# A gated recurrence and a multiplicative FFN on one core: the bf16 cast moves from VectorE to GpSimd, and the second half of the output copy from VectorE to ScalarE

## The chip, the core and the metric

The kernel runs on one core of a Trainium2 chip. The core has five engines that each work through a list of instructions in order and meet only at semaphores: TensorE (matmuls; PE in the profile, and PEld for its weight loads), VectorE (DVE), ScalarE (ACT), GpSimd (POOL) and SyncE (SP, which here only issues transfers). Sixteen DMA engines move data between the device memory (DRAM) and the on-chip SBUF. TensorE writes its results into a second on-chip memory, PSUM, from which VectorE or ScalarE have to copy them out. The metric is the time of one execution on the device in microseconds (us), lower being better.

## What is computed

A recurrence over the sequence, with learned gates, and then a feed-forward block without an activation function, whose two input projections are multiplied with each other. Cut to what matters:

```python
# x, r_gate, i_gate: (4, 5824, 256); a_param: (256,); all float32
log_a = 8.0 * sigmoid(r_gate) * np.log(np.clip(sigmoid(a_param), 1e-06, 1.0 - 1e-06))
a_t = np.exp(log_a)
norm = np.sqrt(np.maximum(1.0 - a_t * a_t, 1e-06))
x_gated = norm * sigmoid(i_gate) * x
for t in range(S):
    h = a_t[:, t] * h + x_gated[:, t]
    y[:, t] = h
x = y.reshape(B * S, D)                      # 23296 tokens of 256
out = ((x @ w1) * (x @ w2) @ w3) @ w_out     # d_ff = 1024
```

## The kernel before

The 23296 tokens are cut into 46 chunks: one of 256 tokens, then 45 of 512. A chunk goes through two halves.

The front half makes y, the recurrence's result, with channels on the partitions. `load` fetches the gates r and i and the input x (512 KB each). ScalarE takes the tanh of both gates (`tanh_r`, L95, and `tanh_i`, L104; a sigmoid is half of one plus a tanh). GpSimd makes of the second the gate (L106) and multiplies it with x into u (L107). r's tanh and u are transposed by DMA (L115, issued by SyncE). ScalarE makes the decay a of the transposed tanh (L125, one instruction for each of two channel blocks), GpSimd squares it (L131), ScalarE takes the root of one minus the square (L136). VectorE then does `gated` (L144, root times transposed u), two scans, one for each channel block (L164), and `cast` (L170), which turns the scan's float32 result h into the bf16 tile y that TensorE reads. The tanhs and exps of a group of up to four chunks are done together, and then their roots together; ScalarE's list has a table load (1283 ns in the trace) at each switch between the two.

The second half is the FFN. w3 and w_out are first folded into one matrix wp (`fold`, eight times, near the start; it fetches parts of w3 by transfers that GpSimd issues, L214, transposes them on TensorE, L217, and multiplies). For a chunk, `up` is called four times (mp = 0 to 3): 8 matmuls give pa (x @ w1, L178) and pb (x @ w2, L186), 256 of the 1024 columns at a time; ScalarE copies pa to SBUF as sa (L181), and VectorE multiplies sa with pb, still in PSUM, into g (L190). pa and pb share three PSUM buffers, so the pa of a quarter needs the buffer that g freed two quarters earlier, and a pb the one that sa freed a quarter earlier. `down` is called four times (8 matmuls each, L197), and gives po, two calls to a PSUM tile. `store` copies such a tile to SBUF (ot) and sends it out: the first half of a chunk by ScalarE (L205), the second half by VectorE (L207).

The order is written out by hand. The main loop runs over steps s, four quarters (mp) to a step. A quarter holds `up(s, mp)` and `down(s - 2, mp)`; for chunk s + 2 it holds `gated` (mp 0), a scan (mp 1 and 2) and `cast` (mp 3). At mp 1 comes the first `store` of chunk s - 2, and at mp 0 of the next step, ahead of everything else there, the second. The rest of the front half, for chunks of the group ahead, is spread over the quarters by a list of costs (`queue`). So chunk s + 2 is cast at the end of step s, and TensorE first reads it two steps on, five quarters later. The scan result h has two buffers, y has four, u, and the tanh tiles two or six.

Of the kernel before, what the change touches and what calls it, by code (L numbers as in the profile page):

```python
# [18 lines left out]
def kernel(  # L19
# [12 lines left out]
    nc = tc.nc  # L32
# [48 lines left out]
    T = {}  # L81
# [85 lines left out]

    def cast(c):
        w = sizes[c]
        nc.vector.tensor_copy(out=T["y", c][:, :, :w], in_=T["h", c][:, :, :w])  # L170

    def up(c, mp):
        w = sizes[c]
# [27 lines left out]
    def store(c, j2):  # L201
        n = min(2, sizes[c] // P - 2 * j2)
        ot = ffn.tile([P, 2, D], F32, name="ot", tag="ot")
        if j2 == 0:
            nc.scalar.copy(out=ot[:, :n, :], in_=T["po", c][:, :n, :])  # L205
        else:
            nc.vector.tensor_copy(out=ot[:, :n, :], in_=T["po", c][:, :n, :])  # L207
        t0 = starts[c] + 2 * j2 * P
        nc.sync.dma_start(out=out[t0:t0 + n * P, :].rearrange("(j p) c -> p j c", p=P),
                          in_=ot[:, :n, :])  # L210
# [67 lines left out]
    for s in range(s0, NCH + LAG):  # L278
        for mp in range(4):
            if mp == 0 and 0 <= s - LAG - 1 and sizes[s - LAG - 1] > 2 * P:  # L280
                store(s - LAG - 1, 1)
            if 0 <= s < NCH:
                up(s, mp)
            for mi in folds.get((s, mp), []):
                fold(mi)
            d = s - LAG
            if 0 <= d < NCH and mp < sizes[d] // P:
                down(d, mp)
                if mp == 1:
                    store(d, 0)  # L290
            c = s + LEAD
            if 0 <= c < NCH:
                if mp == 0:
                    gated(c)
                elif mp in (1, 2):
                    scan(c, mp - 1)
                else:
                    cast(c)
            for fn in queue.get((s, mp), []):
                fn()  # L300
            while nloaded < NCH and tanh_at[nloaded] - 6 <= 4 * s + mp:
                load(nloaded)
                nloaded += 1
    store(NCH - 1, 1)


# [28 lines left out]
```

## Time and profile before

| | |
|---|---|
| median of 3 runs | 629.22 us (624.34 to 631.0) |
| the profiled execution | 630.42 us |
| its span, first to last instruction | 628.7 us |
| mean granted TensorE clock | 0.983 |
| read from DRAM, written | 78.91 MB, 23.86 MB |
| first chunk's matmuls of the FFN | at 29.9 us |
| last instruction of GpSimd | ends near 558 us |
| last matmul | ends near 624.6 us |

Rows of the profile are read like this. A group of instructions has its line in the kernel, its engine and operation, the tiles written and read, and a shape; then the count, the busy time in us with the mean of one in ns, and the engine's idle time just before them with what ended it. A row of the timeline has the start in us, the duration in us, the engine and the instruction, and in brackets the idle time before. A row of waits has who waited for whom, the us in total, how often, and the longest. A row of a stretch has the busy us of PE, PEld, DVE, ACT and POOL, with the number of instructions in brackets, then the granted clock, the DMA engines' busy share and the GB/s moved. An instruction that has been started and then cannot go on counts as busy, so busy time is not always work. The start, up to about 130 us, fills the pipeline and folds the weights; from 130 to 570 us both halves run; behind that only the FFN is left.

### The profile page before, as it was taken

The numbers are of one execution on the slowest core, as the hardware profiler recorded it, in microseconds if no ns is written. First come the engines' busy times: TensorE is split into PE (matmuls) and PEld (weight loads), VectorE is DVE, ScalarE is ACT, GpSimd is POOL, SyncE is SP. The second block draws the span as 40 slices with busy tenths as digits, with TensorE's granted clock in tenths as the row PEclk, the third lists the DMA queues.
The fourth block names the chain that finished last, engine by engine and source line by source line (L and its number), as shares of the span: only waits on it lengthen the run. The fifth ranks groups of instructions, "written<-read, shape, count | busy, mean of one in ns | idle before, by whom it ended". The sixth has DMA issues, their size and how long they took to land.

```text
span 628.7 us, 8281 instructions
## 1 busy us (share of the span) xinstructions
PE 505.0 (80%) x3000; PEld 301.7 (48%) x3056; DVE 518.0 (82%) x438; ACT 441.0 (70%) x492; POOL 296.7 (47%) x155
## 2 busy tenths in 40 slices
PE   0000816878899899899899899899899899889997
PEld 0000604445555555555555556456455455556665
DVE  0130423699999999999999999999999999999952
ACT  3456131888779879789789789789699697674442
POOL 3165172196653672772772772763754653430000
PEclk9999976999999999999999999999999999999999
DMA  9979687189969969969969979889789788321113
GB/s 192 282 203 241 155 169 161 31 208 254 306 131 313 254 132 326 224 160 301 227 171 284 215 192 286 192 211 282 178 245 279 147 235 249 98 71 51 51 51 101
DMA packets 196089, 123.51 MB, mean 196 GB/s; under 512 B 100304, under 2 KB 194512, under 8 KB 196048
## 3 DMA queue, kind: packets, MB, share of 16 engines
q1 hardware_dynamic: 193312, 119.30, 73.1%
q0 software_dynamic: 2736, 3.67, 3.8%
q8 instruction: 24, 0.39, 0.3%
q14 instruction: 17, 0.14, 0.1%
HBM read 78.91 MB, written 23.86 MB: 163 GB/s over the span
## 4 chain that ended last, share of the span: by engine, by line
PE 42%; DVE 22%; issue 14%; DMA 9%; SPq 5%; ACT 3%; POOL 3%; DVEq 0%; POOLq 0%; ACTq 0%
PE pa L178 14%; PE po L197 13%; PE pb L186 13%; DVE g_t L190 9%; DVE y_t L170 5%; DMA i_t<-in_i_gate_dram 4%; DVE h_t L164 3%; SPq L87 3%; DVE nrm L144 2%; DVE ot L207 2%; DMA rt<-th_r 2%; DMA w_t<-in_moe_w_dram 2%; SPq L115 1%; POOL u_t L107 1%; DMA r_t<-in_r_gate_dram 1%
## 5 line engine op out<-in xcount | busy, mean ns | idle before, releaser
L181 ACT CAST sa<-pa 128x1024 bf16<-128x1024 f32 (+1 forms) x184 | 183.8, 999 | 125.5 <-PE pa L178 116.1
L190 DVE TENSOR_TENSOR g_t<-sa,pb 128x1024 bf16<-128x1024 bf16 (+1 forms) x184 | 219.3, 1192 | 34.8 <-ACT sa L181 30.1
L178 PE MATMUL pa<-y_t,w_sb 128*128 128x512 bf16 (+1 forms) x707 | 185.5, 380 | 64.3 <-DVE g_t L190 31.0
L186 PE MATMUL pb<-y_t,w_sb 128*128 128x512 bf16 (+1 forms) x709 | 185.6, 380 | 4.3 <-ACT sa L181 2.7
L197 PE MATMUL po<-wp_sb,g_t 128*128 128x256 bf16 x1456 | 187.4, 273 | 0.7
L197 PEld LDWEIGHTS <-g_t 128*128 128x128 bf16 x1456 | 142.5, 98 | 53.6
L106 POOL TENSOR_SCALAR th_i<-th_i 128x1024 f32<-128x1024 f32 (+1 forms) x46 | 64.7, 1406 | 217.9 <-ACT th_i L104 204.0
L164 DVE TENSOR_TENSOR_SCAN h_t<-a_t,h_t,nrm 128x512 f32<-128x512 f32 (+3 forms) x90 | 161.1, 1791 | 0.0
L178 PEld LDWEIGHTS <-w_sb 128*128 128x128 bf16 x736 | 72.5, 99 | 122.2 <-issue 66.3
L131 POOL TENSOR_TENSOR nrm<-a_t 128x1024 f32<-128x1024 f32 (+1 forms) x46 | 111.4, 2431 | 30.2 <-ACT a_t L125 30.2
L107 POOL TENSOR_TENSOR u_t<-th_i,x_t 128x1024 bf16<-128x1024 f32 (+1 forms) x46 | 114.5, 2490 | 5.9 <-DMA x_t<-in_x_dram 2.1
L186 PEld LDWEIGHTS <-w_sb 128*128 128x128 bf16 x736 | 72.7, 99 | 90.3 <-issue 5.6
L125 ACT ACTIVATE a_t<-rt,la 128x512 f32<-128x512 bf16 (+1 forms) x92 | 70.7, 806 | 25.3 <-DMA rt<-th_r 25.3
L144 DVE SCALAR_TENSOR_TENSOR nrm<-nrm,ut 128x1024 f32<-128x1024 f32 (+1 forms) x46 | 59.4, 1291 | 29.8 <-ACT nrm L136 29.8
L170 DVE CAST y_t<-h_t 128x1024 bf16<-128x1024 f32 (+1 forms) x46 | 59.7, 1299 | 0.1
L104 ACT ACTIVATE th_i<-i_t 128x1024 f32<-128x1024 f32 (+1 forms) x46 | 48.3, 1051 | 2.0 <-DMA i_t<-in_i_gate_dram 2.0
L136 ACT ACTIVATE nrm<-nrm 128x1024 f32<-128x1024 f32 (+1 forms) x46 | 48.1, 1051 | 0.9 <-POOL nrm L131 0.7
L95 ACT ACTIVATE th_r<-r_t 128x1024 bf16<-128x1024 f32 (+1 forms) x46 | 48.3, 1051 | 0.2
L205 ACT COPY ot<-po 128x512 f32<-128x512 f32 x46 | 27.0, 586 | 26.3 <-PE po L197 25.7
L217 PE MATMUL ptw<-ident,w_t 128*128 128x128 bf16 x64 | 7.5, 289 | 43.3 <-DMA w_t<-in_moe_w_dram 43.3
L207 DVE COPY ot<-po 128x512 f32<-128x512 f32 x45 | 30.6, 679 | 5.2 <-PE po L197 5.2
L217 PEld LDWEIGHTS <-w_t 128*128 128x128 bf16 x64 | 6.4, 135 | 45.1 <-DMA w_t<-in_moe_w_dram 44.2
(24 smaller groups left out, 84.5 us busy)
## 6 DMA issues: line engine op xcount, KB each, us to landing
out_dram<-ot SPq DMA_DIRECT2D x91, 256.0 KB, 2.6
r_t<-in_r_gate_dram SPq DMA_DIRECT2D x45, 512.0 KB, 4.2
i_t<-in_i_gate_dram SPq DMA_DIRECT2D x45, 512.0 KB, 5.5
x_t<-in_x_dram SPq DMA_DIRECT2D x45, 512.0 KB, 6.5
w_t<-in_moe_w_dram POOLq DMA_DIRECT2D x8, 256.0 KB, 6.4
w_sb<-in_moe_w_dram POOLq DMA_DIRECT2D x2, 512.0 KB, 8.4
rt<-th_r SPq DMA_TRANSPOSE x47, 3.4
ut<-u_t SPq DMA_TRANSPOSE x47, 4.4
```

What stands on the lines that cost most here:

```text
L106: nc.gpsimd.tensor_scalar(t[:, :n, :], t[:, :n, :], 1.0, 0.5, op0=ALU.add, op1=ALU.mult)
L107: nc.gpsimd.tensor_mul(out=u[:, :, :n, :].rearrange("p cb j q -> p j cb q"), in0=t[:, :n, :].rearrange("p j (cb q) -> p j cb q", q=P), in1 ...
L125: nc.scalar.activation(out=T["a", c][:, cb, :w], in_=T["pr", c][:, cb, :w], func=AF.Exp, scale=la4[:, cb:cb + 1], bias=la4[:, cb:cb + 1])
L131: nc.gpsimd.tensor_mul(out=t[:, :, :w], in0=T["a", c][:, :, :w], in1=T["a", c][:, :, :w])
L144: nc.vector.scalar_tensor_tensor(out=T["n", c][:, :, :w], in0=T["n", c][:, :, :w], scalar=1e-3, in1=T["pu", c][:, :, :w], op0=ALU.max, op1 ...
L164: nc.vector.tensor_tensor_scan(T["h", c][:, cb, lo:hi], T["a", c][:, cb, lo:hi], T["n", c][:, cb, lo:hi], init, ALU.mult, ALU.add)
L170: nc.vector.tensor_copy(out=T["y", c][:, :, :w], in_=T["h", c][:, :, :w])
L178: nc.tensor.matmul(out=pa[:, q, :w], lhsT=w1_sb[:, cb, m * P:(m + 1) * P], rhs=T["y", c][:, cb, :w], start=(cb == 0), stop=(cb == NCB - 1))
L181: nc.scalar.copy(out=sa[:, :, :w], in_=pa[:, :, :w])
L186: nc.tensor.matmul(out=pb[:, q, :w], lhsT=w2_sb[:, cb, m * P:(m + 1) * P], rhs=T["y", c][:, cb, :w], start=(cb == 0), stop=(cb == NCB - 1))
L190: nc.vector.tensor_mul(out=T["g", c][:, 2 * mp:2 * mp + 2, :w], in0=sa[:, :, :w], in1=pb[:, :, :w])
L197: nc.tensor.matmul(out=T["po", c][:, j % 2, :], lhsT=T["g", c][:, k, j * P:(j + 1) * P], rhs=wp_sb[:, k, :], start=(k == 0), stop=(k == KD ...
```

## The change

Two instructions change their engine. The cast of the scan result to bf16 goes from VectorE to GpSimd, and the second half of the output tile is copied by ScalarE, as the first half is. No tile, buffer count, size or place in the written order changes. The instruction itself stands at the same place of the program, but now in the list of another engine, behind what that engine has there.

```diff
     def cast(c):
         w = sizes[c]
-        nc.vector.tensor_copy(out=T["y", c][:, :, :w], in_=T["h", c][:, :, :w])
+        nc.gpsimd.tensor_copy(out=T["y", c][:, :, :w], in_=T["h", c][:, :, :w])
...
     def store(c, j2):
         n = min(2, sizes[c] // P - 2 * j2)
         ot = ffn.tile([P, 2, D], F32, name="ot", tag="ot")
-        if j2 == 0:
-            nc.scalar.copy(out=ot[:, :n, :], in_=T["po", c][:, :n, :])
-        else:
-            nc.vector.tensor_copy(out=ot[:, :n, :], in_=T["po", c][:, :n, :])
+        nc.scalar.copy(out=ot[:, :n, :], in_=T["po", c][:, :n, :])
```

The lines behind it move up by three. In the lists of instructions below, a scan (L164) is printed under the operation SCALAR_TENSOR_TENSOR.

VectorE's list for one step in the middle of the kernel, before: from the last product g of a step over the cast, the copy ot, and the next step's products, gating and scans.

```order
L190 TENSOR_TENSOR g_t<-sa,pb 128x1024
L170 CAST y_t<-h_t 128x1024
L207 COPY ot<-po 128x512
L190 TENSOR_TENSOR g_t<-sa,pb 128x1024
L144 SCALAR_TENSOR_TENSOR nrm<-nrm,ut 128x1024
L190 TENSOR_TENSOR g_t<-sa,pb 128x1024
L164 SCALAR_TENSOR_TENSOR h_t<-a_t,h_t,nrm 128x512
L190 TENSOR_TENSOR g_t<-sa,pb 128x1024
L164 SCALAR_TENSOR_TENSOR h_t<-a_t,h_t,nrm 128x512
```

The same step with the change.

```order
L190 TENSOR_TENSOR g_t<-sa,pb 128x1024 x2
L144 SCALAR_TENSOR_TENSOR nrm<-nrm,ut 128x1024
L190 TENSOR_TENSOR g_t<-sa,pb 128x1024
L164 SCALAR_TENSOR_TENSOR h_t<-a_t,h_t,nrm 128x512
L190 TENSOR_TENSOR g_t<-sa,pb 128x1024
L164 SCALAR_TENSOR_TENSOR h_t<-a_t,h_t,nrm 128x512
```

Two of nine instructions of the step are gone, and two products now stand next to each other.

GpSimd's list near the start, before: the squares of chunk 1, the gates of chunks 2 and 3, their squares, and the first transfers of w3 (w_t).

```order
L131 TENSOR_TENSOR nrm<-a_t 128x1024
L106 TENSOR_SCALAR th_i<-th_i 128x1024
L107 TENSOR_TENSOR u_t<-th_i,x_t 128x4x2x128
L106 TENSOR_SCALAR th_i<-th_i 128x1024
L107 TENSOR_TENSOR u_t<-th_i,x_t 128x4x2x128
L131 TENSOR_TENSOR nrm<-a_t 128x1024 x2
L214 DMA w_t<-in_moe_w_dram 128x1024 x2
```

The same place with the change.

```order
L131 TENSOR_TENSOR nrm<-a_t 128x1024
L170 CAST y_t<-h_t 128x2x256
L106 TENSOR_SCALAR th_i<-th_i 128x1024
L107 TENSOR_TENSOR u_t<-th_i,x_t 128x4x2x128
L106 TENSOR_SCALAR th_i<-th_i 128x1024
L107 TENSOR_TENSOR u_t<-th_i,x_t 128x4x2x128
L131 TENSOR_TENSOR nrm<-a_t 128x1024 x2
L170 CAST y_t<-h_t 128x1024
L211 DMA w_t<-in_moe_w_dram 128x1024 x2
```

The casts of chunks 0 and 1 came in, the second of them ahead of the issue of the transfers.

ScalarE's list at a step's border in the middle, with the change: the decays of a quarter, the copy that came in (the first ot row), the next step's first sa, a table load and a root, and at the second quarter the copy that ScalarE made before as well.

```order
L125 ACTIVATE a_t<-rt,la_86 128x512 x2
L204 COPY ot<-po 128x512
L181 CAST sa<-pa 128x1024
L136 ACT_TABLE_LOAD
L136 ACTIVATE nrm<-nrm 128x1024
L181 CAST sa<-pa 128x1024
L204 COPY ot<-po 128x512
```

Before, the first ot row of these seven was not in ScalarE's list; the others stood in the same order.

## The prediction

> **What bounds the kernel now.** I read the page's busy shares and slices first, then the stretches, the groups by shape and the waits of the steady middle, and the timeline where a number needed its neighbours. "Pitch" is the time from one chunk of 512 tokens to the next.
>
> The first fence is the page's busy line and its slices for TensorE and VectorE; the second, the stretches (us, then each engine's busy time and instruction count, granted clock, DMA share, GB/s).
>
> ```profile
> PE 505.0 (80%) x3000; PEld 301.7 (48%) x3056; DVE 518.0 (82%) x438; ACT 441.0 (70%) x492; POOL 296.7 (47%) x155
> ...
> DVE  0130423699999999999999999999999999999952
> ```
>
> ```profile
> 130.00:570.00 440.00, 404.46 (x2401) 238.81 (x2446) 437.34 (x352) 358.46 (x400) 247.19 (x115) 1.00 0.85 219
> ...
> 170.00:530.00 360.00, 333.62 (x1983) 197.24 (x2020) 357.34 (x293) 297.31 (x331) 202.97 (x94) 1.00 0.89 228
> 570.00:600.00 30.00, 29.79 (x183) 18.14 (x186) 28.00 (x27) 12.97 (x15) 0.00 (x0) 1.00 0.15 51
> ```
>
> VectorE's 82% is an average over a start in which it idles and a middle in which it does not: from 130 to 570 us it is busy 437.3 of 440. A chunk loads 64 weight blocks into TensorE (16 + 16 + 32), so 2446 loads are 38.2 chunks, and the pitch there is 440 / 38.2 = 11.51 us. Behind 570 us GpSimd is silent, and TensorE sets its own pace: the weight loads of L178 at two places four quarters apart give it.
>
> ```profile
> 575.69 0.64 PEld L178 LDWEIGHTS <-w_sb 128*128 128x128 bf16 x4
> ...
> 586.09 0.64 PEld L178 LDWEIGHTS <-w_sb 128*128 128x128 bf16 x4
> ```
>
> That is a pitch of 10.40 us with no stall: TensorE's floor. So the middle loses 1.11 us per chunk, 42.4 us in 38.2 chunks, and that is all that this change can win there. The waits of 180 to 540 us say to whom it is lost: TensorE waits for VectorE's product, while ScalarE and GpSimd wait for others.
>
> ```profile
> POOL th_i L106 <- ACT th_i L104: 153.7, 24, 12.3
> ACT sa L181 <- PE pa L178: 43.0, 51, 1.9
> PE pa L178 <- DVE g_t L190: 21.1, 24, 1.7
> ACT ot L205 <- PE po L197: 14.3, 24, 0.7
> ```
>
> **Why VectorE is full.** The groups by shape of the same stretch (count, busy us and mean ns, idle before), then single instructions on the timeline (start, duration).
>
> ```profile
> L190 DVE TENSOR_TENSOR g_t<-sa,pb 128x1024 bf16<-128x1024 bf16 x127 | 152.4, 1200 | 2.7 <-PE po L197 2.1
> ...
> L164 DVE TENSOR_TENSOR_SCAN h_t<-a_t,h_t,nrm 128x512 f32<-128x512 f32 x57 | 109.3, 1917 | 0.0
> ...
> L131 POOL TENSOR_TENSOR nrm<-a_t 128x1024 f32<-128x1024 f32 x32 | 81.6, 2560 | 1.9 <-ACT a_t L125 1.9
> L107 POOL TENSOR_TENSOR u_t<-th_i,x_t 128x1024 bf16<-128x1024 f32 x31 | 79.8, 2574 | 2.6
> ...
> L106 POOL TENSOR_SCALAR th_i<-th_i 128x1024 f32<-128x1024 f32 x31 | 43.1, 1390 | 153.7 <-ACT th_i L104 153.7
> L170 DVE CAST y_t<-h_t 128x1024 bf16<-128x1024 f32 x32 | 42.8, 1336 | 0.0
> L144 DVE SCALAR_TENSOR_TENSOR nrm<-nrm,ut 128x1024 f32<-128x1024 f32 x32 | 40.3, 1261 | 0.0
> ...
> L205 ACT COPY ot<-po 128x512 f32<-128x512 f32 x32 | 18.8, 586 | 14.7 <-PE po L197 14.3
> ```
>
> ```profile
> 304.12 2.35 POOL L107 TENSOR_TENSOR u_t<-th_i,x_t 128x1024 bf16<-128x1024 f32 x1
> 304.23 2.79 DVE L170 CAST y_t<-h_t 128x1024 bf16<-128x1024 f32 x1
> ...
> 306.94 0.68 DVE L207 COPY ot<-po 128x512 f32<-128x512 f32 x1
> 307.54 1.20 DVE L190 TENSOR_TENSOR g_t<-sa,pb 128x1024 bf16<-128x1024 bf16 x1
> 308.67 1.21 DVE L144 SCALAR_TENSOR_TENSOR nrm<-nrm,ut 128x1024 f32<-128x1024 f32 x1
> 309.80 1.21 DVE L190 TENSOR_TENSOR g_t<-sa,pb 128x1024 bf16<-128x1024 bf16 x1
> 310.93 1.27 DVE L164 TENSOR_TENSOR_SCAN h_t<-a_t,h_t,nrm 128x512 f32<-128x512 f32 x1
> 312.13 1.19 DVE L190 TENSOR_TENSOR g_t<-sa,pb 128x1024 bf16<-128x1024 bf16 x1
> ...
> 576.45 0.69 DVE L170 CAST y_t<-h_t 128x1024 bf16<-128x1024 f32 x1
> 577.05 0.69 DVE L207 COPY ot<-po 128x512 f32<-128x512 f32 x1
> ```
>
> The same cast takes 0.69 us where GpSimd is silent and 2.79 us where GpSimd's u_t began 0.11 us ahead of it: it ends 0.55 us behind the end of u_t. The scans do the same: 1.27 us alone, 1.917 us in the mean. So cast, scan and GpSimd's work exclude one another, and the wait is booked as VectorE's busy time. From start to start, unhindered, the steps are 1.13 us for a product, 1.13 for the gating (L144), 1.20 for a scan, 0.60 for the cast (576.45 to 577.05), 0.60 for the copy. Per chunk: 4 x 1.13 + 1.13 + 2 x 1.20 + 0.60 + 0.60 = 9.25 us of own work, and waits of 2 x 0.65 (scans) + 0.65 (cast) + 0.05 (gating) = 2.0. That is 11.25 of the 11.51.
>
> **The change part by part.** *Copy.* VectorE loses 0.60 us per chunk. ScalarE gains 0.586 us: its busy time in the middle rises from 358.5 by 38.2 x 0.586 = 22.4 to 381 us, of some 410 us then. The copy stands first in the new step, ahead of the next sa. It waits for the po matmuls that TensorE runs just ahead of the next pa, so ScalarE would wait for TensorE there anyway; its idle 43.0 + 14.3 us in 360 (1.8 per chunk) is the cover. Without that cover each copy costs its 0.586. The output DMA waits on ScalarE instead, on the same po, and the store frees SyncE's queue no later. The last copy of all is 0.69 - 0.59 = 0.1 us shorter: nothing.
>
> *Cast.* VectorE loses 0.60 + 0.65 us. GpSimd gains a one-input instruction of 1024 elements that no row shows. Nearest rows: the one-input L106, 1.04 us alone (60.01 us, below), 1.39 in the mean; above, u_t with two inputs, 2.35. A cast has one input, so I take 1.04 plus waits. Behind it on GpSimd stand th_i, u_t and the squares, and ScalarE waits for the squares. It waits for the second scan, one quarter earlier in program order; GpSimd stood idle 153.7 us of 360 (4.9 per chunk), which covers it. TensorE needs y_t five quarters later (5 x 2.6 = 13 us), and the scan state's buffer comes round after two chunks. Cost in the middle: nothing directly.
>
> *The scans pay for it.* GpSimd's busy time per chunk goes from 1.39 + 2.57 + 2.56 = 6.5 to some 7.7 us, and the pitch shrinks, so its share goes from 57% to about 72%, and the scans' wait from 0.65 to about 0.82 us. VectorE then needs 8.05 (9.25 less the two steps) + 2 x 0.82 + 0.05 = 9.7 us per chunk. That is under 10.40, so TensorE becomes the bound, less what single long waits break through. The upper end: scans and gating always find GpSimd busy and wait for the mean rest of an instruction. With unhindered 1.04, 2.35, 2.35 and 1.04 that is (1.08 + 5.52 + 5.52 + 1.08) / (2 x 6.78) = 0.97 us each, so 8.05 + 2.9 = 10.96. Between 10.40 and 10.96 I take the middle, 10.7: VectorE's mean is below TensorE's floor, but one scan behind u_t alone costs 2 us, near a whole quarter. Gain: (11.51 - 10.7) x 38.2 = 30.9 us.
>
> A rule speaks against this part. The Trainium skill (Perfetto Trace Analysis, "Optimizing Scalar/DVE Operations") says that moving work between VectorE and GpSimd might not help, since they share a read port; its page SBUF — State Buffer ("Who interferes with whom") calls that an exclusive lock held for the whole instruction. The 2.79 us cast agrees with the lock; the rule's result here would be that of the third rival.
>
> *Start.* GpSimd's queue also issues the loads of w3 for the folding, and TensorE waits for them.
>
> ```profile
> 54.98 1.17 POOL L214 DMA_DIRECT2D w_t<-in_moe_w_dram  x2
> ...
> 60.01 1.04 POOL L106 TENSOR_SCALAR th_i<-th_i 128x1024 f32<-128x1024 f32 x1 [3.86 <-ACT th_i L104]
> 60.55 1.03 PE L217 MATMUL ptw<-ident,w_t 128*128 128x128 bf16 x8 [28.79 <-DMA w_t<-in_moe_w_dram]
> ...
> 85.63 1.13 POOL L214 DMA_DIRECT2D w_t<-in_moe_w_dram  x2
> ...
> 95.70 1.03 PE L217 MATMUL ptw<-ident,w_t 128*128 128x128 bf16 x8 [14.47 <-DMA w_t<-in_moe_w_dram]
> ```
>
> The casts of chunks 1 and 2 now stand ahead of the issues at 54.98 and 85.63, with nothing left to hide them: +2 x 1.04 = 2.1 us (0 if a DMA absorbs it, 4.7 at u_t's price).
>
> Sum: 630.42 (the profiled execution, 1.7 above its span and 1.2 above the median) - 30.9 + 2.1 = 601.6, say **602 us**. Ends of this case: 630.4 - 42.4 + 2.1 = 590 (pitch 10.40) and 630.4 - 21.0 + 4.7 = 614 (10.96).
>
> **The rivals.** *The DMA becomes the bound (0.14).* From 170 to 530 us its share is 0.89 over 2020 / 64 = 31.6 chunks: 10.15 us per chunk at full use, hardly under TensorE's 10.40. If it cannot run above 0.92, the pitch is 11.03 and the time 630.4 - 18.3 + 2.1 = 614. For it: the share. Against it: in the waits above no engine waits for a transfer.
>
> *ScalarE eats the gain (0.09).* It carries 0.586 us more per chunk in a pitch shorter by 0.8, which leaves 1.8 - 0.6 - 0.8 = 0.4 us of idle time. If the last copy always delays the sa behind it by its full 0.586, the pitch falls only by 0.2: 630.4 - 7.6 + 2.1 = 625. Against it: sa has over a microsecond before TensorE needs the buffer it frees.
>
> *The shared access is the bound, and the kernel slows (0.08).* By lengths alone the excluded work per chunk is now GpSimd 1.04 + 2.35 + 2.35, scans 2.54, gating 1.21, cast 0.69: 10.2 us, 88% of 11.51. With the cast at 1.04 instead it is 10.5. If that path fills no further than 88%, the pitch is 11.9, the time 630.4 + 15 + 2 = 647. It turns slower from a cast of 0.69 us up, if the 88% is a ceiling; a cast at u_t's 2.35 would force it (11.84 without a gap). Against it: GpSimd's 153.7 us of waiting for ScalarE, in which it asks for nothing.
>
> **How the numbers follow.** The forecast, 590 to 614, has 0.62; the rivals 0.14, 0.09 and 0.08; 0.07 is left to what I have not seen. The number is that of the forecast. The range, 590 to 620, takes in the DMA case and leaves out the last two and most of the rest, 2 in 10. About 1% (6 us) is what a measurement of this kernel can tell from no change. Faster by more: 0.62 + 0.14 + a third of ScalarE's case + half the rest = 0.83. Within 1%: 0.09. Slower: 0.08.
>
> **What would show it.** VectorE's busy time falls from 518 to about 440 (less 59.7 and 30.6, plus 90 x 0.17 of waits); ScalarE's rises to 467; GpSimd's to some 350. The cast on GpSimd has a mean near 1.2 us; a mean over 2 makes me wrong. The middle's pitch is 10.4 to 11.0, and TensorE's waits for g_t shrink. The scans' mean rises from 1.92 to about 2.1; above 2.4 the third rival is at work. Waits for loads or transposes on ScalarE would speak for the DMA, waits of pb for sa for ScalarE. The fold's matmuls start some 2 us later.

## The result, and the profile after

| | before | changed |
|---|---|---|
| median of the runs on one chip | 627.5 us (4 runs, 624.34 to 631.0) | 604.35 us (4 runs, 603.42 to 604.79) |
| ratio, 95% interval | | 0.963 (0.957 to 0.969) |
| profiled execution, its span | 630.42, 628.7 us | 604.79, 602.9 us |

602 us were forecast, 590 to 620 the range. The forecast started from the profiled execution of the kernel before, 630.42 us, and took off 28.8 us; measured are 23.2 us between the medians and 25.6 us between the two profiled executions. The page's busy line and VectorE's slices of the changed kernel:

```profile
PE 503.1 (83%) x3056; PEld 302.3 (50%) x3056; DVE 459.5 (76%) x347; ACT 460.2 (76%) x537; POOL 360.1 (60%) x201
...
DVE  0120333699799899999998998998998998988741
```

The stretches, with the same columns as before (busy us of PE, PEld, DVE, ACT, POOL; clock; DMA share; GB/s):

```profile
130.00:170.00 40.00, 34.70 (x208) 20.09 (x207) 36.11 (x24) 34.17 (x41) 32.16 (x17) 1.00 0.97 257
170.00:520.00 350.00, 340.41 (x2081) 203.37 (x2080) 327.88 (x234) 317.52 (x372) 259.28 (x130) 1.00 0.89 238
...
130.00:545.00 415.00, 400.11 (x2442) 238.62 (x2441) 386.86 (x274) 371.55 (x435) 302.53 (x153) 1.00 0.86 231
545.00:575.00 30.00, 30.00 (x185) 17.91 (x183) 23.61 (x20) 14.98 (x18) 3.12 (x3) 1.00 0.16 53
```

VectorE is no longer full: 327.9 us of 350. The pitch from 130 to 545 us is 415 / (2441 / 64) = 10.88 us, where it was 11.51 from 130 to 570; from 170 to 520 us it is 350 / (2080 / 64) = 10.77. The first 40 us won nothing (207 weight loads, 210 before): there the DMA share is 0.97 (1.00 before the change, in the same 40 us).

Groups by shape from 180 to 520 us, and the waits of 180 to 540 us:

```profile
L190 DVE TENSOR_TENSOR g_t<-sa,pb 128x1024 bf16<-128x1024 bf16 x127 | 151.5, 1203 | 21.4 <-ACT sa L181 13.5 <-PE po L197 7.3
...
L164 DVE TENSOR_TENSOR_SCAN h_t<-a_t,h_t,nrm 128x512 f32<-128x512 f32 x58 | 128.7, 2219 | 0.0
...
L106 POOL TENSOR_SCALAR th_i<-th_i 128x1024 f32<-128x1024 f32 x31 | 50.3, 1622 | 47.6 <-ACT th_i L104 47.6
...
L144 DVE SCALAR_TENSOR_TENSOR nrm<-nrm,ut 128x1024 f32<-128x1024 f32 x31 | 42.0, 1354 | 0.0
L170 POOL CAST y_t<-h_t 128x1024 bf16<-128x1024 f32 x31 | 39.1, 1260 | 38.1 <-DVE h_t L164 29.5 <-PE pb L186 8.5
L204 ACT COPY ot<-po 128x512 f32<-128x512 f32 x64 | 37.1, 579 | 17.8 <-PE po L197 14.5 <-DMA out_dram<-ot 2.9
```

```profile
PE pa L178 <- DVE g_t L190: 9.5, 15, 1.1
...
DVE g_t L190 <- ACT sa L181: 14.2, 17, 1.1
...
ACT sa L181 <- PE pa L178: 14.4, 31, 1.0
...
POOL th_i L106 <- ACT th_i L104: 48.6, 10, 5.9
POOL y_t L170 <- DVE h_t L164: 36.0, 10, 6.5
```

The cast costs GpSimd 1.26 us. The scans wait longer: a scan of 512 columns takes 2.22 us in the mean from 180 to 520 us, where it took 1.89 in the same stretch before. VectorE now waits for ScalarE at times, which it did not before, and TensorE's waits for VectorE fell from 21.1 to 9.5 us. So the picture is in outline the forecast one: VectorE is no longer full, and TensorE is the bound with some stalls left.

### The profile page after: what moved, and what is told of

The parts are those of the page before. It is cut to its first block, busy times and chain, and to the rows that moved or that the text cites. A ratio compares the mean times of both kernels' runs of the same rounds, so it can differ in the third digit from the quotient of the medians.

```text
span 602.9 us, 8389 instructions
## 1 busy us (share of the span) xinstructions
PE 503.1 (83%) x3056; PEld 302.3 (50%) x3056; DVE 459.5 (76%) x347; ACT 460.2 (76%) x537; POOL 360.1 (60%) x201
## 4 chain that ended last, share of the span: by engine, by line
PE 55%; ACT 12%; issue 11%; DVE 7%; POOL 7%; DMA 5%; SPq 3%; ACTq 0%; POOLq 0%; DVEq 0%
PE po L197 18%; PE pa L178 18%; PE pb L186 17%; ACT sa L181 5%; DVE g_t L190 5%; ACT a_t L125 3%; SPq L87 3%; POOL nrm L131 3%; DMA rt<-th_r 2%; POOL u_t L107 2%; DVE h_t L164 1%; DMA w_t<-in_moe_w_dram 1%; POOL th_i L106 1%; ACT th_i L104 1%; PE pw L220 1%
## 5 line engine op out<-in xcount | busy, mean ns | idle before, releaser
L178 PE MATMUL pa<-y_t,w_sb 128*128 128x512 bf16 (+1 forms) x736 | 189.6, 381 | 49.3 <-POOL y_t L170 36.5
L186 PE MATMUL pb<-y_t,w_sb 128*128 128x512 bf16 (+1 forms) x736 | 189.4, 380 | 5.5 <-ACT sa L181 5.4
L164 DVE TENSOR_TENSOR_SCAN h_t<-a_t,h_t,nrm 128x512 f32<-128x512 f32 (+3 forms) x90 | 182.4, 2028 | 0.0
L106 POOL TENSOR_SCALAR th_i<-th_i 128x1024 f32<-128x1024 f32 (+1 forms) x46 | 71.8, 1560 | 91.8 <-ACT th_i L104 81.6
L107 POOL TENSOR_TENSOR u_t<-th_i,x_t 128x1024 bf16<-128x1024 f32 (+1 forms) x46 | 116.7, 2537 | 5.9 <-DMA x_t<-in_x_dram 2.1
L170 POOL CAST y_t<-h_t 128x1024 bf16<-128x1024 f32 (+1 forms) x46 | 56.2, 1221 | 81.6 <-DVE h_t L164 70.6
L144 DVE SCALAR_TENSOR_TENSOR nrm<-nrm,ut 128x1024 f32<-128x1024 f32 (+1 forms) x46 | 62.4, 1357 | 29.9 <-ACT nrm L136 29.9
L204 ACT COPY ot<-po 128x512 f32<-128x512 f32 x91 | 52.8, 580 | 32.5 <-PE po L197 29.1
L220 PE MATMUL pw<-wo_sb,w3t 128*128 128x256 bf16 x64 | 13.4, 382 | 6.8 <-DVE w3t L217 6.8
```

The source lines that it names most:

```text
L106: nc.gpsimd.tensor_scalar(t[:, :n, :], t[:, :n, :], 1.0, 0.5, op0=ALU.add, op1=ALU.mult)
L107: nc.gpsimd.tensor_mul(out=u[:, :, :n, :].rearrange("p cb j q -> p j cb q"), in0=t[:, :n, :].rearrange("p j (cb q) -> p j cb q", q=P), in1 ...
L144: nc.vector.scalar_tensor_tensor(out=T["n", c][:, :, :w], in0=T["n", c][:, :, :w], scalar=1e-3, in1=T["pu", c][:, :, :w], op0=ALU.max, op1 ...
L164: nc.vector.tensor_tensor_scan(T["h", c][:, cb, lo:hi], T["a", c][:, cb, lo:hi], T["n", c][:, cb, lo:hi], init, ALU.mult, ALU.add)
L170: nc.gpsimd.tensor_copy(out=T["y", c][:, :, :w], in_=T["h", c][:, :, :w])
L178: nc.tensor.matmul(out=pa[:, q, :w], lhsT=w1_sb[:, cb, m * P:(m + 1) * P], rhs=T["y", c][:, cb, :w], start=(cb == 0), stop=(cb == NCB - 1))
```

## The experiments

### Each part alone

First: the copy on ScalarE, the cast back on VectorE.

```diff
-        nc.gpsimd.tensor_copy(out=T["y", c][:, :, :w], in_=T["h", c][:, :, :w])
+        nc.vector.tensor_copy(out=T["y", c][:, :, :w], in_=T["h", c][:, :, :w])
```

> The cast is back on VectorE; only the output copy's second half is on ScalarE. If VectorE's full list is what the change relieved (my theory): own work 9.25 - 0.60 = 8.65 us per chunk, waits 2.0 as before, the 0.26 us that stayed unexplained before: a pitch near 10.9 us, some 22 us gained, 606 us, ratio 0.966. If the copy was worth nothing and the cast brought all: the time of before, ratio 1.00. If the copy brought all: 604 us, ratio 0.963, and the run with the cast alone is no faster than before.

Second: the cast on GpSimd, the copy's second half back on VectorE.

```diff
-        nc.scalar.copy(out=ot[:, :n, :], in_=T["po", c][:, :n, :])
+        if j2 == 0:
+            nc.scalar.copy(out=ot[:, :n, :], in_=T["po", c][:, :n, :])
+        else:
+            nc.vector.tensor_copy(out=ot[:, :n, :], in_=T["po", c][:, :n, :])
```

> The copy's second half is back on VectorE; only the cast is on GpSimd. My theory: own work 8.65 us per chunk, scans' waits 2 x 0.95 as in the changed kernel, gating 0.13, unexplained 0.26: pitch 10.9 to 11.0 us, 20 us gained, 607 us, ratio 0.968. The two parts alone then gain more in sum (some 42 us) than together (23 us), since TensorE's floor cuts the second. If the cast only trades its own wait for the scans': ratio 0.99 to 1.00. If it brings all: 604 us.

Measured: the copy alone 623.94 us, ratio 0.997 (0.994 to 1.000); the cast alone 619.66 us, 0.991 (0.988 to 0.993). The theory that was written down for these runs was wrong: it wanted 606 and 607. The parts gain 0.3% and 0.9% apart and 3.7% together.

VectorE is still nearly full in both (347.7 before; 344.4 and 345.1 of 350 us from 170 to 520). So the time taken off came back on VectorE itself. The groups by shape of the two, 180 to 520 us, the copy alone first:

```profile
L164 DVE TENSOR_TENSOR_SCAN h_t<-a_t,h_t,nrm 128x512 f32<-128x512 f32 x54 | 108.9, 2016 | 0.0
...
L144 DVE SCALAR_TENSOR_TENSOR nrm<-nrm,ut 128x1024 f32<-128x1024 f32 x30 | 44.9, 1496 | 0.0
L170 DVE CAST y_t<-h_t 128x1024 bf16<-128x1024 f32 x30 | 40.9, 1364 | 0.0
```

```profile
L164 DVE TENSOR_TENSOR_SCAN h_t<-a_t,h_t,nrm 128x512 f32<-128x512 f32 x55 | 114.7, 2086 | 0.0
...
L144 DVE SCALAR_TENSOR_TENSOR nrm<-nrm,ut 128x1024 f32<-128x1024 f32 x30 | 62.4, 2080 | 0.0
```

The same waits by place in the step, from the single instructions of full size that begin between 160 and 520 us on the timeline: mean duration less that of an unhindered one (1.27 us for a scan, 1.21 for the gating, 0.69 for the cast).

| wait, us per chunk | first scan | second scan | cast | gating | sum | own work removed |
|---|---|---|---|---|---|---|
| before | 0.08 | 1.22 | 0.74 | 0.00 | 2.03 | |
| copy alone | 0.00 | 1.51 | 0.71 | 0.29 | 2.51 | 0.60 |
| cast alone | 0.14 | 1.49 | none | 0.87 | 2.51 | 0.60 |
| both | 0.81 | 1.10 | none | 0.14 | 2.05 | 1.20 |

Either part takes 0.60 us of work off VectorE, and 0.48 us of it come back as waiting. That leaves 0.12 us; the pitch from 170 to 520 us fell by 0.06 and 0.13 (11.44 before, 11.38 and 11.31 us). With both, the waits are back at 2.05. The timeline of the kernel with the copy alone shows how a wait can stretch:

```profile
305.82 1.27 DVE L164 TENSOR_TENSOR_SCAN h_t<-a_t,h_t,nrm 128x512 f32<-128x512 f32 x1
306.24 1.70 POOL L106 TENSOR_SCALAR th_i<-th_i 128x1024 f32<-128x1024 f32 x1 [2.55 <-ACT th_i L104]
...
307.02 1.19 DVE L190 TENSOR_TENSOR g_t<-sa,pb 128x1024 bf16<-128x1024 bf16 x1
...
308.02 2.36 POOL L107 TENSOR_TENSOR u_t<-th_i,x_t 128x1024 bf16<-128x1024 f32 x1
308.13 3.33 DVE L164 TENSOR_TENSOR_SCAN h_t<-a_t,h_t,nrm 128x512 f32<-128x512 f32 x1
...
310.34 2.81 POOL L131 TENSOR_TENSOR nrm<-a_t 128x1024 f32<-128x1024 f32 x1
...
311.39 1.19 DVE L190 TENSOR_TENSOR g_t<-sa,pb 128x1024 bf16<-128x1024 bf16 x1
312.50 1.20 DVE L170 CAST y_t<-h_t 128x1024 bf16<-128x1024 f32 x1
```

ScalarE releases th_i, which stands behind the first scan (1.70 in place of 1.04 us). u_t follows, and starts 0.11 us ahead of the second scan, which is held for nearly the whole of it. The square then stands behind the scan, and the cast behind the square. GpSimd and VectorE go through the chunks in a fixed order. In this stretch, where VectorE arrives earlier it waits longer, for an end that ScalarE's release of th_i has set. The order and the waits repeat every four chunks, the group in which ScalarE takes the tanhs and the roots. Here are the second scans of the four chunks before those lines:

```profile
262.47 3.33 DVE L164 TENSOR_TENSOR_SCAN h_t<-a_t,h_t,nrm 128x512 f32<-128x512 f32 x1
...
273.66 3.32 DVE L164 TENSOR_TENSOR_SCAN h_t<-a_t,h_t,nrm 128x512 f32<-128x512 f32 x1
...
285.42 1.27 DVE L164 TENSOR_TENSOR_SCAN h_t<-a_t,h_t,nrm 128x512 f32<-128x512 f32 x1
...
294.96 3.15 DVE L164 TENSOR_TENSOR_SCAN h_t<-a_t,h_t,nrm 128x512 f32<-128x512 f32 x1
```

The next three take 3.33, 3.32 and 1.27 us again, and so it goes on through the middle, except where a scan is cut in two because one of the four sequences ends in its chunk. The kernel before and the changed one repeat in the same way, each with its own pattern. So these waits are no random draw over GpSimd's busy share, as the prediction had them: that share is 0.57 before and 0.58 with the copy alone, and the waits rose from 2.03 to 2.51 us.

### Is it the length of GpSimd's instructions?

If so, the same work in shorter pieces must let the parts pay. u_t and the square are cut in two, one instruction for each channel block:

```diff
-        nc.gpsimd.tensor_mul(out=u[:, :, :n, :].rearrange("p cb j q -> p j cb q"),
-                             in0=t[:, :n, :].rearrange("p j (cb q) -> p j cb q", q=P),
-                             in1=T["x", c][:, :n, :].rearrange("p j (cb q) -> p j cb q", q=P))
+        for cb in range(NCB):
+            nc.gpsimd.tensor_mul(out=u[:, cb, :n, :], in0=t[:, :n, cb * P:(cb + 1) * P],
+                                 in1=T["x", c][:, :n, cb * P:(cb + 1) * P])
...
-        nc.gpsimd.tensor_mul(out=t[:, :, :w], in0=T["a", c][:, :, :w], in1=T["a", c][:, :, :w])
+        for cb in range(NCB):
+            nc.gpsimd.tensor_mul(out=t[:, cb, :w], in0=T["a", c][:, cb, :w],
+                                 in1=T["a", c][:, cb, :w])
```

On the kernel before:

> The kernel before with u_t and squares cut in two. Own work 9.25 us per chunk on VectorE and waits of some 1.0 in place of 2.0: pitch 10.5 to 10.9 us, 600 to 612 us, if the length of GpSimd's instructions is what VectorE's waits come from. If not, 625 us.

On the kernel with the copy alone:

> The kernel with the copy alone moved (cast on VectorE), and GpSimd's u_t and squares each cut into two instructions of half the size, one for each channel block: the same work, held half as long at a time. The two parts of the change alone gained 0.3% and 0.9%, since the time taken off VectorE came back as waits for GpSimd: the second scan stands 2.0 us behind u_t in three chunks of four. If that is what kept the parts from paying, that wait falls to 1.0 us or less, the pitch to 10.5 to 10.8 us, the time to 596 to 608 us. If something else holds this kernel at 11.35 us (the DMA, ScalarE's order), it stays at 622 to 626 us.

On the kernel with the cast alone:

> The kernel with the cast alone moved to GpSimd (copy on VectorE), and u_t and squares cut in two. With short GpSimd instructions the parts should pay one by one: the split kernel of before takes 606.8 us, with the copy moved 598.1, with both 592.8. If the waits no longer stretch: 595 to 600 us. If the cast pays only together with the copy whatever the length: 605 us or more.

On the changed kernel:

> The changed kernel with u_t and squares cut in two. Its pitch from 170 to 530 us is 10.78 us, 0.38 above TensorE's 10.40. If these 0.38 us are single long waits behind GpSimd's instructions: pitch 10.45 to 10.6, 592 to 599 us. If they are the DMA's or ScalarE's: 604 us as before, or some more, for GpSimd's extra 92 instructions.

| | GpSimd whole | GpSimd in halves |
|---|---|---|
| neither part | 625 to 628 us | 606.76 us, 0.968 (0.963 to 0.974) |
| copy alone | 623.94 us, 0.997 | 598.07 us, 0.955 (0.949 to 0.960) |
| cast alone | 619.66 us, 0.991 | 590.74 us, 0.943 (0.939 to 0.946) |
| both | 604.35 us, 0.963 | 592.79 us, 0.945 (0.939 to 0.952) |

The stretch of 170 to 520 us, four kernels in halves: neither part, the copy, the cast, both.

```profile
170.00:520.00 350.00, 339.98 (x2065) 201.63 (x2063) 348.06 (x298) 302.22 (x337) 241.69 (x162) 1.00 0.92 238
```

```profile
170.00:520.00 350.00, 347.22 (x2124) 207.52 (x2123) 344.29 (x273) 321.93 (x379) 256.20 (x166) 1.00 0.94 242
```

```profile
170.00:520.00 350.00, 349.49 (x2148) 209.86 (x2146) 342.58 (x276) 311.69 (x349) 290.72 (x203) 1.00 0.93 242
```

```profile
170.00:520.00 350.00, 349.65 (x2150) 210.21 (x2149) 320.08 (x243) 324.75 (x384) 291.92 (x201) 1.00 0.93 243
```

Halving alone, with not a microsecond of work moved, gives nearly what the change gives. VectorE's waits, by the same reading as in the table above, are 1.47, 1.66, 1.52 and 1.31 us per chunk in these four kernels, against 2.03, 2.51, 2.51 and 2.05 with whole instructions. With halves each part pays by itself, and they no longer need each other; beside the cast, the copy brings nothing more. With the cast moved TensorE is at its floor: 350 / (2146 / 64) = 10.44 us and, with both, 10.42, where 10.40 was read from the end of the kernel before. So the 0.37 us that the changed kernel stays above the floor from 170 to 520 us go as well when GpSimd's instructions are cut. Halving also changes when each of them starts, and no run holds the starts fixed, so length and timing are not told apart here. The DMA at a share of 0.93 lets TensorE run at its floor, which rules the DMA out as the bound of the changed kernel in this stretch (share 0.89). The two fastest kernels cannot be told apart, and both beat the changed one.

Cutting u_t alone, on the kernel with the copy alone:

> The kernel with the copy alone moved, and u_t alone cut in two; the squares stay whole. If the second scan's 2.0 us behind u_t are most of what keeps this kernel at 624 us: 604 us or less, most of the way to the 598 us of both cut. If the squares (behind which cast and gating wait) matter as much: about half way, 611 us. If u_t does not matter: 620 us or more.

607.68 us, 0.968 (0.962 to 0.975), over runs that spread from 602 to 611. That lies between two of the three answers (604 and 611): u_t carries most of the gain, the squares the last 10 us.

### Does the cast cost anything on GpSimd?

A cast can be left out, since the scan can write y in bf16 itself. The state that passes from one chunk to the next is then rounded to bf16.

```diff
-        T["h", c] = ypool.tile([P, NCB, CT], F32, name="h_t", tag="h")
         T["y", c] = ypool.tile([P, NCB, CT], BF16, name="y_t", tag="y", bufs=4)
+        T["h", c] = T["y", c]
...
-                else:
-                    cast(c)
```

With the copy on ScalarE, as in the changed kernel:

> The changed kernel without any cast: the scan writes y in bf16 itself, and the next chunk starts from the last bf16 column. VectorE's list is that of the changed kernel, GpSimd's is 1.2 us per chunk shorter. If the cast costs something on GpSimd (by waits of the gating and scans behind it): pitch 10.5 to 10.7, 594 to 602 us. If GpSimd's idle time hides it: 604 us within 1.

With the copy on VectorE:

> No cast at all (the scan writes y in bf16), copy on VectorE: VectorE's list is that of the kernel with the cast alone moved (619.7 us), but GpSimd has no cast. If time taken off VectorE comes back as waits behind u_t and the squares, whether or not GpSimd has a cast: 614 to 622 us. If the cast alone gains so little because of what it adds on GpSimd: 604 us or less.

595.39 us, 0.952 (0.946 to 0.958), and 595.28 us, 0.951 (0.946 to 0.956). The first says that the cast on GpSimd is not free: without it the kernel is some 7 to 9 us faster (by the ratios and by the medians; the two intervals just touch). About 3 us of this come from 170 to 520 us, where the pitch is 350 / (2100 / 64) = 10.67 in place of 10.77, and about 3 us from the 40 us before, with 224 weight loads in place of 207. The waits hardly change in sum, 1.96 in place of 2.05 us per chunk: the scans wait less and the gating more. Of the two answers for the second run, the one that blames the cast on GpSimd came, and by more than it asked. VectorE's list is that of the kernel with the cast alone (619.66 us), and the time is 24 us lower. So the cast alone gains so little because of what it does on GpSimd: there, by the same reading of the timeline, the second scan meets u_t in 22 of 29 chunks, here in 15 of 31, and waits 0.99 in place of 1.49 us. The scan and the gating without a cast, from 180 to 520 us (2086 and 2080 ns with the cast alone, above):

```profile
L164 DVE TENSOR_TENSOR_SCAN y_t<-a_t,y_t,nrm 128x512 bf16<-128x512 f32 x58 | 107.4, 1851 | 0.0
...
L144 DVE SCALAR_TENSOR_TENSOR nrm<-nrm,ut 128x1024 f32<-128x1024 f32 x32 | 57.0, 1782 | 0.0
```

The waits do not always come back; it depends on what GpSimd starts in between. And without a cast, moving the copy brings nothing.

The opposite: a second cast on GpSimd, into a tile that nobody reads.

```diff
+        spare = ypool.tile([P, NCB, CT], BF16, name="y2_t", tag="y2")
+        nc.gpsimd.tensor_copy(out=spare[:, :, :w], in_=T["h", c][:, :, :w])
```

> The changed kernel with a second cast of the same scan result on GpSimd, into a tile that nobody reads: 1.04 us more per chunk that excludes VectorE's scans. By the exclusion as waits (my theory): the scans' mean rises from 2.0 to about 2.2 us, VectorE stays under TensorE's floor in the mean, the pitch rises by 0.1 to 0.3 us: 608 to 616 us. If GpSimd's spare time covers it: 604 us. If the excluded work is a ceiling that was already reached (third rival): the whole 1.04 x 38 = 40 us, 644 us.

614.37 us, 0.981 (0.977 to 0.986): the pitch rises by 0.34 us, from 10.77 to 350 / (2017 / 64) = 11.11. The size is as expected, the way to it is not: the scans' mean fell to 1.93 us and the gating's rose to 1.77, and the waits in sum are 1.88 us per chunk, less than the 2.05 without the second cast. The waits from 180 to 520 us show another path: ScalarE now waits for GpSimd's squares, and VectorE for ScalarE.

```profile
DVE g_t L192 <- ACT sa L183: 34.1, 32, 3.1
ACT nrm L136 <- POOL nrm L131: 20.7, 8, 2.9
```

The excluded work was no ceiling that the changed kernel had reached, or the second cast would have cost 40 us.

A memset in its place, which takes nearly as long and reads nothing from SBUF:

```diff
+        spare = ypool.tile([P, NCB, CT], F32, name="y2_t", tag="y2")
+        nc.gpsimd.memset(spare[:, :, :w], 0.0)
```

> The changed kernel with a memset of a tile of 1024 float32 that nobody reads behind each cast on GpSimd, in place of the second cast of the double-cast kernel (614.4 us): an instruction of about 1 us that reads nothing from SBUF. If any GpSimd instruction keeps VectorE's scans waiting: 610 to 618 us and scans and gating that wait behind it. If only instructions that read do, as the Trainium skill's page SBUF — State Buffer says of two-input VectorE instructions (Who interferes with whom): 604 to 607 us.

599.01 us, 0.956 (0.952 to 0.960): not slower, if anything faster than the changed kernel (the two intervals overlap slightly). The timeline of this kernel shows a scan beside a memset and then one beside a square (the profile prints the spare tile y2 as y_t):

```profile
306.79 0.95 POOL L172 MEMSET y_t<- 128x1024 f32 x1
307.00 1.27 DVE L164 TENSOR_TENSOR_SCAN h_t<-a_t,h_t,nrm 128x512 f32<-128x512 f32 x1
307.70 2.26 POOL L131 TENSOR_TENSOR nrm<-a_t 128x1024 f32<-128x1024 f32 x1
...
309.34 1.70 DVE L164 TENSOR_TENSOR_SCAN h_t<-a_t,h_t,nrm 128x512 f32<-128x512 f32 x1
```

The scan beside the memset takes its unhindered 1.27 us and the memset 0.95 (0.950 us in the mean of 33 from 180 to 520 us); the scan that meets the square waits for it. So it goes throughout: from 170 to 520 us all 15 whole scans that begin beside a memset take 1.27 us. In the kernel with the second cast, all 15 whole scans that begin beside a cast wait for its end and take 1.82 to 2.09 us, for example:

```profile
225.07 1.04 POOL L172 CAST y_t<-h_t 128x1024 bf16<-128x1024 f32 x1
225.28 1.90 DVE L164 TENSOR_TENSOR_SCAN h_t<-a_t,h_t,nrm 128x512 f32<-128x512 f32 x1
```

This agrees with the Trainium skill (SBUF — State Buffer, "Who interferes with whom"), which says that a VectorE instruction with two SBUF inputs contends with GpSimd instructions that read SBUF, not with those that only write. That useless work did not cost anything fits waits that hang on the sequence: in the lines above the memset holds the square back while the scan gets in. That this is why the time fell is not shown.

### The start

The casts of the first three chunks back on VectorE:

```diff
+        eng = nc.vector if c <= 2 else nc.gpsimd
-        nc.gpsimd.tensor_copy(out=T["y", c][:, :, :w], in_=T["h", c][:, :, :w])
+        eng.tensor_copy(out=T["y", c][:, :, :w], in_=T["h", c][:, :, :w])
```

> The changed kernel with the casts of chunks 0, 1 and 2 back on VectorE, so that none stands ahead of the issue of the w3 transfers on GpSimd. If the start term of the prediction is real: 2 us less than the changed kernel, 602 us. If the transfers absorb it: the same 604 us within 0.5.

602.97 us, 0.964 (0.959 to 0.969), over six runs from 600.8 to 606.8: no difference can be told from 604.35. A term of 2.1 us would not stand out from that spread, so the trace of the changed kernel at the place is read as well:

```profile
54.28 1.04 POOL L170 CAST y_t<-h_t 128x1024 bf16<-128x1024 f32 x1
55.26 1.18 POOL L211 DMA_DIRECT2D w_t<-in_moe_w_dram  x2
...
82.02 1.03 POOL L170 CAST y_t<-h_t 128x1024 bf16<-128x1024 f32 x1
...
84.86 1.14 POOL L211 DMA_DIRECT2D w_t<-in_moe_w_dram  x2
```

```profile
59.11 1.03 PE L214 MATMUL ptw<-ident,w_t 128*128 128x128 bf16 x8 [20.75 <-DMA w_t<-in_moe_w_dram]
...
93.32 1.03 PE L214 MATMUL ptw<-ident,w_t 128*128 128x128 bf16 x8 [13.54 <-DMA w_t<-in_moe_w_dram]
```

The casts stand there at 1.04 us as priced, but the issues are 0.28 us later and 0.77 us earlier than before, and the fold's matmuls come 1.4 and 2.4 us earlier. When the transfers land moves by more than the casts from trace to trace: the last fold's matmuls end between 102.2 and 111.4 us in the fourteen kernels of this document, in no order of where the cast is (111.4 before, 109.3 with the change, 108.5 with the three casts back).

## Why the prediction was right

*The bound.* VectorE full, and TensorE's floor 10.40 us behind it: right. Halves show 10.42 as the floor under load.

*The middle.* Forecast pitch 10.7 us over all of it; measured 10.88, of which the first 40 us stayed as they were and the rest, 375 us with 2441 - 207 = 2234 loads, ran at 10.74. The gain of 30.9 us was so too large, in part by the 40 us at a DMA share near 1 in which nothing was won; the kernels in halves win next to nothing there either (198 to 213 weight loads, 210 before). From 170 to 520 us alone the pitch fell from 11.44 to 10.77. The 10.7 was no result of the sum: it was taken as the middle of 10.40 and 10.96. That the measured pitch came so near to it is in part luck, since the same way of reckoning missed by 13 and 18 us when the parts were run alone.

*The copy's and the cast's price.* The step "VectorE loses 0.60" and "0.60 + 0.65 us" failed as a term for each part. VectorE's waits were priced as a share of GpSimd's busy time, which would make the removed work a gain wherever VectorE is full. The runs showed that they belong to a sequence that repeats, and that 0.48 of 0.60 us come back when one part is made. The forecast held because both were made: 1.20 us of work went, and the waits stayed at 2.05. Why the sequence with both parts has no more waiting than before, and that with either part has 0.48 us more, is not settled; the memset shows that a shift in GpSimd's timing can change it. One length was wrong as well: the square was priced at 2.35 us, but unhindered it takes 1.88 (in the kernel before at 83.80 us), and 2.35 has a wait in it. By the prediction's own sum the upper end of the pitch would then be 10.7 in place of 10.96.

*The cast on GpSimd.* 1.26 us measured, 1.04 plus waits forecast: right. "Cost in the middle: nothing directly" was right for TensorE and ScalarE, but this kernel is 7 to 9 us slower than the one without a cast, of which some 6 us can be placed (half in the first 40 us of the middle, half in a pitch longer by 0.1) and their cause is open.

*The scans pay for it.* Forecast mean 2.1 us, measured 2.18 from 180 to 540 us, the stretch of the 1.92 before: a wait of 0.91 us in place of the forecast 0.82. The gating waits 0.14 in place of 0.05. VectorE's total was forecast at 440 us and came out at 459.5, ScalarE's was forecast at 467 and came out at 460, GpSimd's at 350 and 360.

*ScalarE's copy.* Hidden from TensorE, as forecast: it waits for sa in no row of the middle, and ScalarE's copies, old and new, wait 15.2 us for po. It is not without effect, though: VectorE waits for sa, 14.2 us in the changed kernel where it waited in no row before, and in the kernels in halves with the cast moved 27.4 us with the copy on ScalarE and 0.2 with it on VectorE (180 to 520 us). VectorE has that time to spare.

*The start.* 2.1 us were added that no run showed. The fold's matmuls were to start some 2 us later and came 1.4 and 2.4 us earlier, and with the first casts back on VectorE no change can be told.

*The rivals.* The DMA: ruled out by the floor reached at a share of 0.93. ScalarE: ruled out by the kernel with both parts and halves, which carries its copy at a pitch of 10.42. The shared access as a ceiling at 88%: ruled out by the second cast, which cost 10 us, not 40. By the prediction's count of unhindered lengths, with the square at 1.88 us, the excluded work was 9.7 of 11.44 us (85%) before and is 10.1 of 10.77 (93%) with the change. With the second cast it is 11.1 of 11.11 us; whether the access itself is the limit there, no run tells. Its weaker form, that moving work from VectorE to GpSimd might not help (the Trainium skill, Perfetto Trace Analysis, "Optimizing Scalar/DVE Operations"), came close to true for the cast alone with whole instructions, 0.9%.

## What to carry to other kernels

Where two engines exclude one another, a busy share of 99% can hide much waiting (here 2.0 of 11.4 us, nearly a fifth). List each instruction by its shortest duration first, and treat the rest as a wait that may grow when work is taken away. Look for the longest instruction on the other engine and cut it: here halving two GpSimd instructions gave 3% without moving anything, and made each part pay by itself. Price a change of two parts also part by part, by a run of each, before crediting either.

## What was not expected of the hardware

A GpSimd memset of 0.95 us ran beside a scan without a wait on either side, while GpSimd's cast, product and square, of 1.0 to 2.4 us, each held scans that began behind them until their end. And 46 such memsets, 43 us of additional work on GpSimd, left the kernel at 599.0 us where it was 604.35 without them.
